# Attention, MoE and softplus MLP on one core: six late weight pieces every four units, second GEMM four units behind, abs ahead of gh

## The chip, the cores and the metric

The program runs on one core of one Trainium2 chip. The metric is device time in microseconds (us); lower is better. Five engines work side by side, each through its own list in order: PE (TensorE, matmuls; its weight loads are listed as PEld), DVE (VectorE), ACT (ScalarE), POOL (GpSimd) and SP, which here only issues DMAs.

## The reference, cut to what matters

Windowed attention, then a mixture of eight experts (the first MoE), then a dense MLP with softplus between its two GEMMs. The change lies in that last part, called the second MoE by the code.

```python
def _moe2_ref(x, w_in, w_out):          # x 2304x512, w_in 512x2048, w_out 2048x512
    h = x @ w_in
    g = np.maximum(h, 0.0) + np.log1p(np.exp(-np.abs(h)))
    return (g @ w_out).astype(np.float32)

def _moe_ref(x, w_gate, w_output_gate, w1, w2):
    ...
    for e in range(E):                  # 8 experts, a token goes to its best one
        ...
        h = np.maximum(x[mask] @ w1[e], 0.0)
        ye = h @ w2[e]
        out[mask] = gate_w[mask, None] * eom[mask, e, None] * ye
```

w_in and w_out arrive as 64-bit floats. The kernel reads them as pairs of 32-bit words and makes 32-bit floats of them with integer operations.

## The kernel before

**Precision.** Every GEMM is done with three matmuls: each operand is cut into a high part (a cast on ACT, names wh, gh, xh) and a low part (a subtraction on DVE, names wl, gl, xl), and high x high, high x low and low x high are summed in PSUM.

**Second MoE.** The 2304 tokens stand in 6 blocks b of 384, the 2048 hidden columns in 16 strips f of 128. A pair (b, f) is a unit; the list `steps` has 96 of them, blocks 0 and 1 interleaved in groups of four strips (units 0 to 31), blocks 2 to 5 after them. In the loop, round i issues on PE `gemm1` of unit i (12 matmuls of 384 columns into one of two buffers of PSUM, pg) and `gemm2` of unit i - LAG (9 matmuls of 512 columns into q); LAG is 3. Between them stands softplus, in three pieces, recorded in the order c of unit i - 2, a of unit i, b of unit i - 1:

- `softplus_a` (L1394): ACT takes u = |h| (L1399), u = exp(-u) (L1400) and l = relu(h) (L1401), the two reads of pg; DVE takes w = u + 1 (L1402) and the rounding error of that sum, u = (w - 1) - u (L1404).
- `softplus_b` (L1406): ACT takes w = ln w (L1408), DVE l = l + w (L1409) and l = l - u (L1411).
- `softplus_c` (L1415): ACT casts gh from l (L1417), DVE subtracts gl = l - gh (L732).

**Weights.** w_in and w_out of the second MoE come in 16 pieces of 128 x 1024: even pieces hold two strips of w_in, odd ones those of w_out. Pieces 0 to 7 are made 32-bit during the first MoE (`prep_tick`, every fifth step of experts 1 to 7, one 128 x 512 slice at a time: a load, |w| on ACT, four operations on DVE, a store), stored in DRAM as w_in32 and w_out32, and read back. Then they need a cast `hi_` and a subtraction `lo_` of 128 x 1024 each, at the unit that N_HL gives (16 there is unit 0). Pieces 8 to 15 are late: they are loaded as 64-bit words into two tiles wr each and converted during units 2 to 27 by `direct` in four steps, piece j at unit D_AT + D_STEP * (j - 8) + D_OFF[step]: steps 0 and 1 are |w| of one half on ACT into a tile cm (L168; the pool cm has one buffer), then four operations on DVE (L172, L178, L180, L182), put between the softplus operations by `aside`; step 2 casts both halves to wh on ACT (L816); step 3 subtracts wl, two halves, on POOL (L732 there).

**Buffers.** wr has five tiles. `load_next` issues the next load on SP when a piece's low part has been recorded; a late piece needs two tiles. Finished rows of q are copied to o by DVE or ACT and scattered to the output by an indirect DMA from POOL (L1440). After the last gemm1, END orders the matmuls of gemm2 that are left by strip and by third t of the block: before, the first third of block 5 is finished nine matmuls before the end, the second six, the last third at the end.

Of the kernel before, what the change touches and what calls it, by code (L numbers as in the profile page):

```python
# [21 lines left out]
P = 128  # L22
# [5 lines left out]
WARM = 28  # L28
NE_AT = ((6, 14), (7, 0), (7, 1), (7, 2))
X2_AT, X2_HL = (0, 3), ((6, 7, 8, 9), (12, 13, 14, 15))  # L30
N_HL = (8, 10, 12, 14, 16, 18, 20, 22)

D_AT, D_STEP, D_OFF = 2, 3, (0, 1, 3, 4)
XG = 6
IDX_AT, GATHER_AT = 8, 12
TR_AT = (5, 7, 8, 9)
# [6 lines left out]
def attn_moe_softplus_kernel(ctx: ExitStack, tc: tile.TileContext, q, k, v, w_gate, w_ogate, w1, w2, w_in, w_out, out, dbg=None):  # L43
# [25 lines left out]
    identb = const.tile([P, P], BF16, name="identb")  # L69
    upper = const.tile([P, P], BF16, name="upper")  # L70
    ones = const.tile([P, P], BF16, name="ones")
    wg = const.tile([P, NC, 32], F32, name="wg")
    rev = const.tile([P, NE], F32, name="rev")
    eidx = const.tile([P, NE], F32, name="eidx")
    ebase = const.tile([P, NE], BF16, name="ebase")
    pair = const.tile([P, NTL, 2], I32, name="pair")
    lg = const.tile([P, NTL, 2 * NE], F32, name="lg")
    cumb = const.tile([P, len(GROUPS) + 1, NE], BF16, name="cumb")
    tabi = const.tile([1, 40], I32, name="tabi")
    perm_sb = const.tile([P, NT // P, 2], I32, name="perm_sb")  # L80
# [69 lines left out]


    DIRECT = 8
    N_IN, N_OUT = DIRECT // 4, DIRECT // 4 * (PC // P)
    PREP = [(0, r_, c_) for r_ in range(DM // P) for c_ in range(N_IN)] + [(1, r_, 0) for r_ in range(N_OUT)]
    NPREP = len(PREP)
    prep_in, prep_t, prep_n = {}, {}, [0, 0, 0]
# [588 lines left out]
    pieces = {}  # L745

    def load_piece(r, j, e=None):
        if r == NE and j >= DIRECT:

            pieces[r, j] = []  # L750
            for h in range(2):
                if j % 2 == 0:
                    src = w_in.bitcast(I32)[256 * h : 256 * h + 256, 256 * j : 256 * j + 512].rearrange("(c p) f -> p c f", p=P)
                else:
                    src = w_out.bitcast(I32)[128 * (j - 1 + h) : 128 * (j - 1 + h) + 128].unsqueeze(1)
                t = K["wr"].tile([P, 1024], F32, tag="wr", name=f"wr{r}_{j}{h}").bitcast(I32)
                nc.sync.dma_start(t.rearrange("p (c f) -> p c f", c=src.shape[1]), src)
                pieces[r, j].append(t)
            return
        if r == NE:  # L760
            g = j // 2
            if j % 2 == 0:
                src = w_in32[:, 256 * g : 256 * g + 256].rearrange("(c p) f -> p c f", p=P)
            else:
                src = w_out32[256 * g : 256 * g + 256].rearrange("(c p) d -> p c d", p=P)
        elif j < 4:
            src = w1[ds(e, 1), :, 256 * j : 256 * j + 256].rearrange("o (c p) f -> p (o c) f", p=P)
        else:
# [27 lines left out]
    def direct(j, step):  # L796
# [18 lines left out]
            for h in range(2):  # L815
                nc.scalar.copy(d[2][:, hs[h]], w_[h])  # L816
        else:
            for h in range(2):
                sub(nc.gpsimd, d[3][:, hs[h]], w_[h], d[2][:, hs[h]])
                load_next()  # L820

    def piece_lo(r, j, eng=None):
        d = pieces[r, j]
# [215 lines left out]
    def load_next():  # L1039

        nload[1] += 1
        while nload[1] and nload[0] < len(order_):
            r, j = order_[nload[0]]
            two = r == NE and j >= DIRECT
            if two and nload[1] < 2:
                break
            if r not in er and r != NE:
# [259 lines left out]
        sub(nc.vector, x2[b][1][:, cs, :BT], x2[b, h], x2[b][0][:, cs, :BT])  # L1307


    for j, u in enumerate(N_HL):  # L1310
        last_rank.setdefault(u, []).append((hi_, NE, j))
        last_rank.setdefault(u + 1, []).append((lo_, NE, j))
    for b, at_ in enumerate(X2_HL):
# [59 lines left out]

    cctx = mctx
    K["wb"] = cctx.enter_context(tc.tile_pool(name="wb", bufs=1))
    K["cm"] = cctx.enter_context(tc.tile_pool(name="cm", bufs=1))
    sp_p = cctx.enter_context(tc.tile_pool(name="sp", bufs=2))
    g_p = cctx.enter_context(tc.tile_pool(name="g", bufs=3))
    o_p = cctx.enter_context(tc.tile_pool(name="o", bufs=3))
# [15 lines left out]
    def softplus_a(b, f):  # L1395
# [3 lines left out]
        nc.scalar.activation(u, ps, AF.Abs)  # L1399
        nc.scalar.activation(u, u, AF.Exp, scale=-1.0)  # L1400
        nc.scalar.activation(l, ps, AF.Relu)  # L1401
        nc.vector.tensor_scalar(w_, u, 1.0, None, ALU.add)  # L1402
        aside()
        nc.vector.scalar_tensor_tensor(u, w_, 1.0, u, ALU.subtract, ALU.subtract)  # L1404

    def softplus_b(b, f):  # L1406
        u, w_, l = sp[b, f]
        nc.scalar.activation(w_, w_, AF.Ln)  # L1408
        nc.vector.tensor_tensor(l, l, w_, ALU.add)  # L1409
        aside()  # L1410
# [113 lines left out]
```

## Time and profile before

| | |
|---|---|
| median of 3 runs (lowest, highest) | 814.38 us (814.18 to 817.77) |
| the profiled execution's own time | 815.12 us |
| its span in the trace | 813.5 us |
| busy in the span: PE, DVE, ACT, POOL | 95%, 70%, 58%, 17% |
| mean granted clock of PE | 0.981 |
| first MoE, first gemm to last | 158.6 to 390.7 us |
| second MoE, first gemm1 to last matmul | 390.8 to 802.9 us |

PE is named busy for 95% of the span, but its matmuls are pipelined and their ends are modelled, so a busy share hides small waits. A stretch is better read by how many matmuls began in it: the same 21 matmuls (12 and 9) make a unit all through the second MoE. The count behind PEld, one weight load for each matmul, serves for that.

### The profile page before, as it was taken

The page shows a single profiled execution, that of the slowest core. Times are in us where ns is not written, and L with a number is a line of the kernel's source. Part 1 is how long each engine was busy: PE and PEld are TensorE (multiplying, and loading weights), DVE is VectorE, ACT ScalarE, POOL GpSimd, SP SyncE. Part 2 cuts the span into 40 slices and gives each one's busy share as a digit, 9 for nine tenths or more (in the row PEclk, how much of TensorE's full clock was granted, in tenths as well). Part 3 has the DMA queues.
Part 4 walks back from the last instruction along what each step waited for, and adds up shares of the span by engine and source line. Part 5 has one row for each costly group of instructions (what it writes and reads, how often), then busy time and mean ns, then how long its engine had stood idle before and what let it go on. Part 6 is the DMA issues. An engine that isn't in the chain of part 4 may idle for free.

```text
span 813.5 us, 14993 instructions
## 1 busy us (share of the span) xinstructions
PE 769.4 (95%) x5542; PEld 689.8 (85%) x5543; DVE 566.0 (70%) x1112; ACT 471.8 (58%) x909; POOL 141.3 (17%) x170
## 2 busy tenths in 40 slices
PE   6998885999999999999989999999999999999994
PEld 5666664898999999999978888899999999999993
DVE  6867884653577887656798989867656656666662
ACT  4776542344655665566766676656656655655561
POOL 9814433121102001100012121210000001001001
PEclk8999998799999999999999999999999999999998
DMA  9996666255799998769431322310000001001000
GB/s 227 267 249 172 137 163 154 72 194 168 241 285 294 306 306 281 234 195 345 109 103 62 96 67 71 91 65 1 20 7 33 0 1 39 1 1 39 1 1 39
DMA packets 85887, 104.49 MB, mean 128 GB/s; under 512 B 30428, under 2 KB 61404, under 8 KB 85792
## 3 DMA queue, kind: packets, MB, share of 16 engines
q1 hardware_dynamic: 74496, 84.22, 35.9%
q0 software_dynamic: 5104, 13.40, 5.1%
q10 hardware_dynamic: 6192, 5.56, 2.0%
q8 instruction: 65, 1.06, 0.6%
q14 instruction: 30, 0.25, 0.1%
HBM read 83.98 MB, written 19.32 MB: 127 GB/s over the span
## 4 chain that ended last, share of the span: by engine, by line
PE 61%; DVE 11%; issue 9%; ACT 4%; DMA 2%; POOL 1%; ACTq 0%; POOLq 0%; DVEq 0%; SPq 0%
PE q L1433 5%; PE pg L895 5%; PE pg L896 5%; PE pg L894 5%; PE q L1431 5%; PE q L1432 5%; PE ph L890 3%; PE ph L892 3%; PE ph L891 3%; PE py L890 3%; PE py L891 3%; PE py L892 3%; DVE l L1411 2%; DVE l L1409 1%; PE py L894 1%
## 5 line engine op out<-in xcount | busy, mean ns | idle before, releaser
L895 PE MATMUL pg<-xlm,wh 128*128 128x384 f32 x384 | 129.7, 338 | 0.0
L894 PE MATMUL pg<-xhm,wh 128*128 128x384 f32 x384 | 129.4, 337 | 0.1
L896 PE MATMUL pg<-xhm,wl 128*128 128x384 f32 x384 | 129.3, 337 | 0.0
L1433 PE MATMUL q<-wh,gl 128*128 128x512 f32 x288 | 114.3, 397 | 3.8 <-DVE gl L732 3.8
L1431 PE MATMUL q<-wh,gh 128*128 128x512 f32 x288 | 114.2, 397 | 1.4 <-ACT gh L1417 0.9
L1432 PE MATMUL q<-wl,gh 128*128 128x512 f32 x288 | 113.2, 393 | 0.0
L732 DVE TENSOR_TENSOR wl<-wr,wh 128x1024 fp32r<-128x1024 f32 x72 | 87.6, 1218 | 32.9 <-ACT wh L787 32.9
L1417 ACT CAST gh<-l 128x384 fp32r<-128x384 f32 x96 | 49.2, 512 | 100.9 <-DVE l L1411 100.9
L732 DVE TENSOR_TENSOR gl<-l,gh 128x384 fp32r<-128x384 f32 x96 | 56.6, 590 | 41.2 <-ACT gh L1417 39.6
L787 ACT CAST wh<-wr 128x1024 fp32r<-128x1024 f32 x72 | 75.0, 1047 | 15.2 <-ACT y L917 6.0
L894 PEld LDWEIGHTS pg<-xhm,wh 128*128 128x128 f32 x384 | 72.1, 188 | 4.3 <-ACT l L1401 0.4
L895 PEld LDWEIGHTS pg<-xlm,wh 128*128 128x128 f32 x384 | 72.0, 188 | 3.8
L1433 PEld LDWEIGHTS q<-wh,gl 128*128 128x128 f32 x288 | 54.0, 188 | 22.1 <-DVE gl L732 10.1
L1402 DVE TENSOR_SCALAR w<-u 128x384 f32<-128x384 f32 x96 | 34.7, 361 | 54.5 <-ACT u L1400 53.8
L896 PEld LDWEIGHTS pg<-xhm,wl 128*128 128x128 f32 x384 | 72.1, 188 | 0.0
L1440 POOL DMA_INDIRECT out_dram<-o,perm_sb x18 | 18.6, 1034 | 271.9 <-DVE o L259 137.4
L1431 PEld LDWEIGHTS q<-wh,gh 128*128 128x128 f32 x288 | 54.1, 188 | 11.9 <-ACT gh L1417 4.2
L1411 DVE TENSOR_TENSOR l<-l,u 128x384 f32<-128x384 f32 x96 | 62.2, 648 | 2.8
L1432 PEld LDWEIGHTS q<-wl,gh 128*128 128x128 f32 x288 | 54.1, 188 | 8.2
L1399 ACT ACTIVATE u<-pg 128x384 f32<-128x384 f32 x96 | 46.9, 488 | 22.3 <-PE pg L896 21.9
L890 PE MATMUL ph<-xh,wh 128*128 128x392 f32 (+5 forms) x192 | 58.5, 305 | 0.9 <-ACT y L917 0.9
L890 PE MATMUL py<-hh,wh 128*128 128x312 f32 (+8 forms) x192 | 58.5, 304 | 0.0
(205 smaller groups left out, 1763.6 us busy)
## 6 DMA issues: line engine op xcount, KB each, us to landing
wr<-in_moe_w_dram SPq DMA_DIRECT2D x64, 512.0 KB, 5.3
raw<-in_q_dram SPq DMA_DIRECT2D x8, 576.0 KB, 5.8
raw<-in_k_dram SPq DMA_DIRECT2D x8, 576.0 KB, 7.5
x2r<-yT_dram SPq DMA_DIRECT2D x12, 384.0 KB, 3.6
vP<-in_v_dram SPq DMA_DIRECT2D x16, 272.0 KB, 8.3
praw<-in_moe_w_in_dram SPq DMA_DIRECT2D x8, 512.0 KB, 5.0
praw<-in_moe_w_out_dram SPq DMA_DIRECT2D x8, 512.0 KB, 5.5
wr<-in_moe_w_in_dram SPq DMA_DIRECT2D x8, 512.0 KB, 4.0
```

Source lines behind the costliest of these rows:

```text
L732: e.tensor_tensor(lo, src, hi.bitcast(F32), ALU.subtract)
L787: (eng or nc.scalar.copy)(d[1], d[0])
L890: nc.tensor.matmul(ps if wide else ps[:, :cut], wh, xh if wide else xh[:, :cut], start=wide, stop=False, skip_group_check=True)
L891: nc.tensor.matmul(ps[:, :cut], wh, xl[:, :cut], start=False, stop=False, skip_group_check=True)
L894: nc.tensor.matmul(ps, wh, xh, start=(first and i == 0), stop=False)
L895: nc.tensor.matmul(ps, wh, xl, start=False, stop=False)
L896: nc.tensor.matmul(ps, wl, xh, start=False, stop=(last and i == k - 1))
L1411: nc.vector.tensor_tensor(l, l, u, ALU.subtract)
L1417: nc.scalar.copy(gT[b, f][0], l)
L1431: nc.tensor.matmul(acc[b, t], gh[:, ts_], wh, start=(f == 0), stop=False)
L1432: nc.tensor.matmul(acc[b, t], gh[:, ts_], wl, start=False, stop=False)
L1433: nc.tensor.matmul(acc[b, t], gl[:, ts_], wh, start=False, stop=(f == NF - 1))
```

## The change

- Pieces 9 and 11 are no longer late. N_OUT rises by four, so four more 128 x 512 slices of w_out go through `prep_tick` in the first MoE; the two pieces are then read from w_out32 and split by `hi_` and `lo_` at units 8 and 14. Late are the six pieces 8, 10, 12, 13, 14, 15, one every four units from unit 4 on, their last two steps in the same round.
- cm has two buffers. Room comes from wg and lg, which move from the pool const to a pool that closes after the attention.
- The two subtractions of wl of a late piece go from POOL to DVE, one `aside` each.
- w = u + 1 is done on ACT (a copy with a bias of 1) for the first 28 units, on DVE after.
- l = l - u is taken in `softplus_a`, ahead of the logarithm.
- The order within a round is a, c, b: |h| stands in front of gh. LAG is 4, and END is written anew: the first third of block 5 is finished twelve matmuls before the end, the second still six.

```diff
-N_HL = (8, 10, 12, 14, 16, 18, 20, 22)
-D_AT, D_STEP, D_OFF = 2, 3, (0, 1, 3, 4)
+N_HL = {0: 8, 1: 10, 2: 12, 3: 14, 4: 16, 5: 18, 6: 20, 7: 22, 9: 24, 11: 30}
+D_AT, D_STEP, D_OFF = 4, 4, (0, 1, 3, 3)
...
-    N_IN, N_OUT = DIRECT // 4, DIRECT // 4 * (PC // P)
+    N_IN, N_OUT = DIRECT // 4, DIRECT // 4 * (PC // P) + 4
+    LATE = [j for j in range(DIRECT, 16) if j not in (9, 11)]
...
-            for h in range(2):
-                sub(nc.gpsimd, d[3][:, hs[h]], w_[h], d[2][:, hs[h]])
-                load_next()
+            def subs():
+                for h in range(2):
+                    sub(nc.vector, d[3][:, hs[h]], w_[h], d[2][:, hs[h]])
+                    load_next()
+                    yield 1
+            side.append(subs())
...
-    K["cm"] = cctx.enter_context(tc.tile_pool(name="cm", bufs=1))
+    K["cm"] = cctx.enter_context(tc.tile_pool(name="cm", bufs=2))
+    LAG = 4
...
         nc.scalar.activation(l, ps, AF.Relu)
-        nc.vector.tensor_scalar(w_, u, 1.0, None, ALU.add)
+        if steps.index((b, f)) < 28:
+            nc.scalar.activation(w_, u, AF.Copy, bias=1.0)
+        else:
+            nc.vector.tensor_scalar(w_, u, 1.0, None, ALU.add)
         aside()
         nc.vector.scalar_tensor_tensor(u, w_, 1.0, u, ALU.subtract, ALU.subtract)
+        aside()
+        nc.vector.tensor_tensor(l, l, u, ALU.subtract)
 
     def softplus_b(b, f):
         u, w_, l = sp[b, f]
         nc.scalar.activation(w_, w_, AF.Ln)
         nc.vector.tensor_tensor(l, l, w_, ALU.add)
-        aside()
-        nc.vector.tensor_tensor(l, l, u, ALU.subtract)
         aside()
...
-    LAG = 3
-    END = {0: [(NF - 3, (0, 1)), (NF - 2, (0, 1)), (NF - 3, (2,))], 2: [(NF - 1, (0, 1)), (NF - 2, (2,)), (NF - 1, (2,))]}
+    END = {0: [(NF - 4, (0, 1, 2)), (NF - 3, (0, 1)), (NF - 2, (0,)), (NF - 3, (2,))], 2: [(NF - 1, (0,)), (NF - 2, (1,)), (NF - 1, (1,)), (NF - 2, (2,)), (NF - 1, (2,))]}
...
-            order_sp = [(2, softplus_c), (0, softplus_a), (1, softplus_b)]
+            order_sp = [(0, softplus_a), (2, softplus_c), (1, softplus_b)]
```

**ACT while a late piece is converted.** In the names, u0_5 is u of block 0, strip 5, cm10_1 is |w| of the second half of piece 10, pg the result of gemm1. Before, from one half's |w| to the next:

```order
L168 ACTIVATE cm10_0_8827<-wr8_100_8735 128x512
L1417 CAST gh1_3_8851<-l1_3_8774 128x384
L1399 ACTIVATE u0_5_8856<-pg0_5_8829 128x384
L1400 ACTIVATE u0_5_8856<-u0_5_8856 128x384
L1401 ACTIVATE l0_5_8858<-pg0_5_8829 128x384
L1408 ACTIVATE w0_4_8813<-w0_4_8813 128x384
L168 ACTIVATE cm10_1_8876<-wr8_101_8737 128x512
L1417 CAST gh0_4_8900<-l0_4_8814 128x384
```

The same piece of ACT's list now:

```order
L167 ACTIVATE cm10_0_8842<-wr8_100_8750 128x512
L1406 ACTIVATE u0_5_8871<-pg0_5_8849 128x384
L1407 ACTIVATE u0_5_8871<-u0_5_8871 128x384
L1408 ACTIVATE l0_5_8873<-pg0_5_8849 128x384
L1410 ACTIVATE w0_5_8872<-u0_5_8871 128x384
L1427 CAST gh1_3_8882<-l1_3_8778 128x384
L1420 ACTIVATE w0_4_8824<-w0_4_8824 128x384
L167 ACTIVATE cm10_1_8890<-wr8_101_8752 128x512
```

The cast gh of the unit two back stood first in a round, ahead of the reads of pg; it now stands behind them and behind the new sum w.

**DVE at the end of a late piece.** Before, DVE's list where piece 8 is being finished (its wl is on POOL) and piece 9 begins:

```order
L732 TENSOR_TENSOR gl1_0_8715<-l1_0_8629,gh1_0_8714 128x384
L172 TENSOR_SCALAR cm9_0_8687<-cm9_0_8687 128x512
L1402 TENSOR_SCALAR w1_2_8720<-u1_2_8719 128x384
L178 TENSOR_SCALAR cm9_0_8687<-cm9_0_8687 128x512
L1404 SCALAR_TENSOR_TENSOR u1_2_8719<-w1_2_8720,u1_2_8719 128x384
L1409 TENSOR_TENSOR l1_1_8674<-l1_1_8674,w1_1_8673 128x384
L180 SCALAR_TENSOR_TENSOR wr8_90_8642<-wr8_90_8642,cm9_0_8687 128x512
L1411 TENSOR_TENSOR l1_1_8674<-l1_1_8674,u1_1_8672 128x384
L182 SCALAR_TENSOR_TENSOR wr8_90_8642<-wr8_90_8642 128x512
```

Now, where piece 8 is finished and piece 9, prepared, is split:

```order
L733 TENSOR_TENSOR wl8_8_8792<-wr8_80_8526,wh8_8_8791 128x512
L1414 SCALAR_TENSOR_TENSOR u0_4_8823<-w0_4_8824,u0_4_8823 128x384
L733 TENSOR_TENSOR wl8_8_8792<-wr8_81_8528,wh8_8_8791 128x512
L1416 TENSOR_TENSOR l0_4_8825<-l0_4_8825,u0_4_8823 128x384
L733 TENSOR_TENSOR gl1_2_8837<-l1_2_8732,gh1_2_8836 128x384
L1421 TENSOR_TENSOR l1_3_8778<-l1_3_8778,w1_3_8777 128x384
L733 TENSOR_TENSOR wl8_9_8796<-wr8_9_8586,wh8_9_8795 128x1024
```

The two wl of piece 8 came onto DVE, the sum w left it, and l = l - u moved up by a round.

**DVE at the border of two experts of the first MoE.** pw18 is slice 18 of `prep_tick`, wl6_3 a low weight of expert rank 6, hl6_0 the low part of its first hidden strip, which frees that strip's buffer of PSUM. Before, DVE's list there:

```order
L732 TENSOR_TENSOR wl6_3_7267<-wr6_3_6827,wh6_3_7266 128x1024
L908 SCALAR_TENSOR_TENSOR hl6_0_7401<-ph6_0_7374,hh6_0_7400 128x280
L732 TENSOR_TENSOR wl6_4_7372<-wr6_4_6932,wh6_4_7371 128x1024
L878 UNCONDITIONAL_BRANCH
L908 SCALAR_TENSOR_TENSOR hl6_1_7434<-ph6_1_7407,hh6_1_7433 128x280
```

Now:

```order
L733 TENSOR_TENSOR wl6_3_7285<-wr6_3_6833,wh6_3_7284 128x1024
L177 TENSOR_SCALAR pw17_7107<-pw17_7107 128x512
L179 SCALAR_TENSOR_TENSOR pw17_7107<-praw17_6527,pw17_7107 128x512
L181 SCALAR_TENSOR_TENSOR pw17_7107<-praw17_6527,pw17_7107 128x512
L171 TENSOR_SCALAR pw18_7333<-pw18_7333 128x512
L177 TENSOR_SCALAR pw18_7333<-pw18_7333 128x512
L179 SCALAR_TENSOR_TENSOR pw18_7333<-praw18_6599,pw18_7333 128x512
L181 SCALAR_TENSOR_TENSOR pw18_7333<-praw18_6599,pw18_7333 128x512
L171 TENSOR_SCALAR pw19_7403<-pw19_7403 128x512
L914 SCALAR_TENSOR_TENSOR hl6_0_7433<-ph6_0_7406,hh6_0_7432 128x280
```

Eight operations of two slices came in a row between the last weights of one expert and the first hidden strip of the next.

## Rows read from the trace of the kernel before

**Rows 1.** Stretches of the second MoE: length, busy us of each engine (instructions)
```profile
core 0: us, PE busy (x) PEld busy (x) DVE busy (x) ACT busy (x) POOL busy (x), PEclk, DMA share, GB/s
401.76:516.89 115.13, 109.91 (x526) 92.64 (x525) 105.26 (x194) 75.47 (x159) 23.20 (x16) 1.00 0.26 79
525.28:792.41 267.13, 267.13 (x1345) 242.62 (x1344) 172.22 (x339) 156.44 (x339) 15.74 (x15) 1.00 0.05 19
700.61:733.70 33.09, 33.09 (x169) 30.26 (x168) 21.64 (x43) 19.28 (x41) 0.00 (x0) 1.00 0.01 1
```

**Rows 2.** Waits from 401.76 to 516.89: who for whom: us, times, longest
```profile
ACT gh L1417 <- DVE l L1411: 24.4, 17, 2.8
ACT cm L168 <- DVE wr L180: 14.2, 8, 1.8
PEld q L1433 <- DVE gl L732: 9.8, 19, 1.3
```

**Rows 3.** DVE's groups in that stretch: xcount | busy us, mean ns | idle before
```profile
L1411 DVE TENSOR_TENSOR l<-l,u 128x384 f32<-128x384 f32 x26 | 23.1, 890 | 0.3
L732 DVE TENSOR_TENSOR gl<-l,gh 128x384 fp32r<-128x384 f32 x25 | 17.0, 682 | 6.1 <-ACT gh L1417 4.5 <-PE pg L896 1.2
L1409 DVE TENSOR_TENSOR l<-l,w 128x384 f32<-128x384 f32 x26 | 15.4, 593 | 0.0
L182 DVE SCALAR_TENSOR_TENSOR wr<-wr 128x512 int32<-128x512 int32 x16 | 10.9, 682 | 0.0
L1402 DVE TENSOR_SCALAR w<-u 128x384 f32<-128x384 f32 x25 | 8.9, 356 | 3.1 <-ACT u L1400 2.7
L172 DVE TENSOR_SCALAR cm<-cm 128x512 f32<-128x512 f32 x16 | 6.7, 418 | 0.0
L732 DVE TENSOR_TENSOR wl<-wr,wh 128x1024 fp32r<-128x1024 f32 x3 | 3.7, 1218 | 0.0
```

**Rows 4.** The first of those groups from 560 to 740 us, without late pieces
```profile
L1411 DVE TENSOR_TENSOR l<-l,u 128x384 f32<-128x384 f32 x44 | 24.5, 557 | 1.5
```

**Rows 5.** ACT's groups in the stretch of rows 1
```profile
L1408 ACT ACTIVATE w<-w 128x384 f32<-128x384 f32 x25 | 12.9, 515 | 0.0
L168 ACT ACTIVATE cm<-wr 128x512 f32<-128x512 f32 x15 | 10.1, 675 | 14.2 <-DVE wr L180 14.2
L816 ACT CAST wh<-wr 128x512 fp32r<-128x512 f32 x16 | 9.7, 657 | 0.0
L787 ACT CAST wh<-wr 128x1024 fp32r<-128x1024 f32 x2 | 2.1, 1047 | 0.0
```

**Rows 6.** Timeline of one late piece: start us, length us, [idle before <-releaser]
```profile
457.75 2.89 POOL L732 TENSOR_TENSOR wl<-wr,wh 128x512 fp32r<-128x512 f32 x2 [10.59 <-ACT wh L816]
457.83 1.66 DVE L1411 TENSOR_TENSOR l<-l,u 128x384 f32<-128x384 f32 x1
463.57 0.68 ACT L168 ACTIVATE cm<-wr 128x512 f32<-128x512 f32 x1 [1.80 <-DVE wr L180]
```

**Rows 7.** Timeline at the start: first two |h|, last matmul of the fourth gemm1
```profile
393.75 0.48 ACT L1399 ACTIVATE u<-pg 128x384 f32<-128x384 f32 x1
395.17 0.49 ACT L1399 ACTIVATE u<-pg 128x384 f32<-128x384 f32 x1
399.33 0.34 PE L896 MATMUL pg<-xhm,wl 128*128 128x384 f32 x1
```

**Rows 8.** Two stretches of the first MoE, columns as in rows 1
```profile
322.00:334.00 12.00, 11.81 (x91) 11.57 (x89) 11.03 (x18) 8.71 (x17) 0.00 (x0) 1.00 0.70 220
347.00:359.00 12.00, 12.00 (x107) 12.00 (x106) 8.16 (x13) 9.24 (x16) 0.00 (x0) 1.00 0.62 193
```

**Rows 9.** Timeline of the last copy and the last two scatters
```profile
802.92 0.58 ACT L1437 COPY o<-q 128x512 f32<-128x512 f32 x1 [1.45 <-PE q L1433]
803.00 0.96 POOL L1440 DMA_INDIRECT out_dram<-o,perm_sb  x1 [0.31 <-issue]
804.27 0.96 POOL L1440 DMA_INDIRECT out_dram<-o,perm_sb  x1 [0.30 <-issue]
```

More of the change, by code (lines that the diff above doesn't have):

```diff
@@ L71, in attn_moe_softplus_kernel @@
     ones = const.tile([P, P], BF16, name="ones")
-    wg = const.tile([P, NC, 32], F32, name="wg")
     rev = const.tile([P, NE], F32, name="rev")
@@ L76, in attn_moe_softplus_kernel @@
     pair = const.tile([P, NTL, 2], I32, name="pair")
-    lg = const.tile([P, NTL, 2 * NE], F32, name="lg")
     cumb = const.tile([P, len(GROUPS) + 1, NE], BF16, name="cumb")
@@ L215, in attn_moe_softplus_kernel @@
     per_p = [None, actx.enter_context(tc.tile_pool(name="per1", bufs=1))]
+    wg = per_p[1].tile([P, NC, 32], F32, name="wg")
+    lg = per_p[1].tile([P, NTL, 2 * NE], F32, name="lg")
     mask_w = per_p[1].tile([P, 2, 64], BF16, name="mask_w")
@@ L747, in load_piece @@
     def load_piece(r, j, e=None):
-        if r == NE and j >= DIRECT:
+        if r == NE and j in LATE:
             pieces[r, j] = []
@@ L1043, in load_next @@
             r, j = order_[nload[0]]
-            two = r == NE and j >= DIRECT
+            two = r == NE and j in LATE
             if two and nload[1] < 2:
@@ L1307, in x2_lo @@
         sub(nc.vector, x2[b][1][:, cs, :BT], x2[b, h], x2[b][0][:, cs, :BT])
-    for j, u in enumerate(N_HL):
+    for j, u in N_HL.items():
         last_rank.setdefault(u, []).append((hi_, NE, j))
@@ L1465, in attn_moe_softplus_kernel @@
         x2_at(b, *((s0 + 8, s0 + 12, s0 + 13, s0 + 13, s0 + 14) if b == 2 else (s0 + 4, s0 + 8, s0 + 9, s0 + 10, s0 + 11)))
-    for j in range(DIRECT, NF):
+    for k_, j in enumerate(LATE):
         for s in range(4):
-            post.setdefault(D_AT + D_STEP * (j - DIRECT) + D_OFF[s], []).append((direct, j, s))
+            post.setdefault(D_AT + D_STEP * k_ + D_OFF[s], []).append((direct, j, s))
     for i in range(len(steps) + LAG):
```

## The prediction

> **What bounds the kernel now.** I read the stretches first, since PE is named busy nearly everywhere. From unit 31 on, 1344 matmuls begin in 267.13 us [rows 1], one every 0.1988 us, 4.17 us for a unit of 21. That is PE's own pace: it has no gap there, and DVE is busy for 172 of the 267 us, ACT for 156. From unit 4 to unit 28, the same count of 525 matmuls (25 units) takes 115.13 us. At the later pace they would take 525 x 0.1988 = 104.4 us. So **10.8 us** are lost there, all of it while late pieces are converted, and all at a granted clock of 1.00. The reader is to see that the busy share would have hidden this: 109.91 of 115.13 us.
>
> Then the waits of that stretch [rows 2]. PE's weight loads wait for gl from DVE; ACT waits for DVE twice over, 24.4 us for l ahead of gh and 14.2 us for the second |w| of a piece, which needs the one buffer cm. Nothing waits for a DMA. So the loop is DVE to ACT to DVE, and DVE is its heavy part: busy for 105.26 us [rows 1] of work that PE would want done in 104.4.
>
> Last, why DVE is that heavy. Its three softplus operations of 128x384 with two operands, 77 of them, took 23.1 + 17.0 + 15.4 = 55.5 us [rows 3]; at the 0.557 us that the same operation takes where no piece is converted [rows 4] they are 42.9. The 12.6 us between lie where POOL subtracts: one of them takes 1.66 us beside POOL's pair of 2.89 [rows 6]. A piece also makes ACT stand 1.80 us for cm [rows 6], with gh, the reads of pg and exp queued behind it.
>
> **The change, part by part.** The sum is made for the profiled execution, 815.12 us, which is 0.74 above the median.
>
> DVE in the stretch. Busy 105.3; off go the 12.6 of POOL's subtractions, 8.9 of w = u + 1 [rows 3], and two of eight pieces, each 4 x 0.418 + 4 x 0.682 = 4.4 (L178 is like L172 and L180 like L182), 8.8 in all. On come twelve subtractions of 128x512: the trace has none on DVE alone, but it lies between 0.557 [rows 4] and half of 1.218 or the 0.682 of L182 [rows 3]; with the last, 8.2. Two more lo_ of 1.218 make 2.4. Sum 85.6 us, 82% of PE's 104.4.
>
> ACT in the stretch. Busy 75.5 [rows 1]; on come 25 sums. A copy with a bias isn't in the trace; the logarithm, from SBUF to SBUF in the same shape, takes 0.515 [rows 5], and no ACT instruction of this shape differs from it much, so 12.9. Off go two pieces of 2 x 0.675 + 2 x 0.657 = 2.7 [rows 5], 5.3; on come two casts of double width, 2.1. Sum 85.2 us, again 82%.
>
> So both fit under PE with a fifth to spare, and what is late next is PE itself. Three edits make the loop loose as well as light: with two buffers cm the 14.2 us go, because a half waits only for the half before the last; gh now stands behind the reads of pg, so its wait no longer delays them; and gemm2 four units behind gives gl a whole round, 4.17 us, more. l - u ahead of the logarithm costs nothing, it is the same operation, and it shortens what follows the logarithm by 0.557. The SP queue carries fewer loads than before; a load waits there for a tile wr, and behind it stands only the next one, needed four units later. I take the 10.8 us as **gone but for 0.5**: units 4 to 11 hold three of the stretch's four hi_ (pieces 6, 7 and 9) beside the conversion of 8 and 10, so ACT has 8 x 3.41 there and nearly 2 more, 29 of 33.4 us, and waits come in bursts. Bounds 0 and 4 for this rest.
>
> The start. PE now does five gemm1 before its first gemm2, and gemm1 of unit 4 needs relu of unit 2. ACT's first |h| begins at 393.75 and the second 1.42 later [rows 7], so three triples take 4.3; two sums and one logarithm between them 3 x 0.515, and hi_ of piece 5 1.0 [rows 5]: relu of unit 2 ends by 400.6, and a little earlier as neighbours overlap; I take 400.4. PE is free at 399.33 + 0.17 = 399.5 [rows 7], so it waits about 0.9. Against the kernel before it begins that gemm1 at 400.4 with nine matmuls (half a unit, 2.1) still owed, where before began it at 401.76 (the bound of the stretch) without: 400.4 + 2.1 - 401.8 = **+0.7** (0 to 1.5).
>
> The first MoE. Four slices more: 4 x 2.2 = 8.8 us of DVE, 4 x 0.68 of ACT [rows 3, 5], and on SP four loads and four stores, with the experts' weight loads queued behind each store's wait for DVE. It falls between 322 and 359 us. The hard place is the border of ranks 5 and 6, where two slices now follow each other on DVE ahead of the first hl; from 347 to 359 DVE would be filled: 8.16 [rows 8] plus two slices less a clamp, 4.0, of 12.0. The trace has this once already, at the border of ranks 4 and 5: DVE 11.03 of 12.00, and PE lost 0.19 [rows 8]. If nothing covered DVE, all 8.8 would show; PE's three buffers of PSUM for these strips cover it, and I take **+0.5** (0 to 2.5).
>
> The end. The last copy ends at 802.92 + 0.58 = 803.50, but its scatter starts at 804.27, because POOL needs 1.27 for each of three [rows 9]. The first third now finishes three matmuls (0.6) earlier, so POOL's three begin as much earlier, and the last starts at about 803.6: **-0.7** (0 to -0.8; more than the copy's end at 803.50 allows it can't be). Before that, nine more matmuls stand in front of the last strip, so softplus of units 94 and 95 stays covered.
>
> The rest, units 31 to 95, changes order only: PE runs there without gaps, whatever ACT does first.
>
> Sum: -10.8 + 0.5 + 0.7 + 0.5 - 0.7 = **-9.8 us**; 815.12 becomes 805.3, and on the scale of the median 814.38 becomes 804.6.
>
> A rule that speaks against one edit stands in the Trainium skill, "ScalarE: Activation LUTs", section "Rules for kernel authors": an add is to be done on VectorE and not on ScalarE. The trace agrees on the size, 0.356 on DVE [rows 3] against 0.515 for a like ACT instruction. By the rule w would stay on DVE, which would then hold 85.6 + 8.9 = 94.5 of 104.4 us, ACT 72.3. What the rule warns of here is the first rival.
>
> **The rivals.**
>
> *ACT becomes the bound, in part.* A unit's ACT work in the stretch is 85.2 / 25 = 3.41 us. If ACT still waits for DVE by some amount in each unit, PE is slowed once that passes 4.17 - 3.41 = 0.76 us; before, it waited (24.4 + 14.2) / 25 = 1.54 [rows 2]. For it speaks that gh still needs l from DVE one round back and that DVE cannot begin a round before ACT has made w. Against it: the wait for cm has lost its cause, and gh's has 1.9 us more, since four instructions now stand in front of it. At 1.0 us a unit, two thirds of the old wait, 25 x 0.24 = 6 us would stay lost in place of the 0.5: 810.1, between 807.5 and 812.
>
> *Slower: ACT's waits stay.* The same place, with ACT's wait undiminished at 1.54: a unit takes 3.41 + 1.54 = 4.95, 25 of them 123.8 us, 8.6 over before, with the other terms (0.7 + 0.5 - 0.7) +9.1: 823.5. It is slower than before from a wait of 1.2 us a unit (115.13 / 25 - 3.41). Only the loop through DVE could keep it, and DVE is to lose a fifth of its load.
>
> *The first MoE pays.* Weight loads of rank 6 and 7 slip behind the four stores, and PE stands for half of the 8.8 us: +4.4 in place of +0.5, 808.5. Against it, PE lost next to nothing with sixteen such slices in ranks 1 to 5.
>
> *The change doesn't do what it says.* If the loss weren't DVE's load but the pace of PE beside busy engines, nothing would come back: +0.5, 814.9. Against it, rows 2 name the waits, and 115.13 / 104.4 is DVE's own share of load.
>
> **How the numbers follow.** Forecast 804.6, chance 0.69: its own range 801.5 to 807.5 comes from the bounds above, and from PE's pace, which isn't the same in all units: 168 matmuls in 33.09 us is 0.1970 [rows 1], so 1.0 us of the stretch and up to 2 of the rest hang on what sets it. ACT in part 0.15; the first MoE 0.05; nothing comes back 0.07; slower 0.04. To hold 8 in 10 the range must reach into the first rival: 800.8 to 810.0. A difference of 0.5% (4.1 us) is about what a measurement can tell here; faster than 810.3 are the forecast, the first MoE's case and more than half of the first rival: 0.84; within 0.5% 0.12; slower 0.04.
>
> **What would show it.** Units 4 to 28 at 4.1 to 4.25 us each, 525 matmuls in 103.5 to 106; no DVE operation of 1.6 us, POOL without work from 400 to 520; ACT's wait for cm gone, and its wait for l under 10 us; DVE and ACT busy for some 82% there; PE's only wait of note before gemm1 of unit 4, under 1.5 us; less than 1 us lost at 347; the last scatter within 0.2 us of the last copy. I am wrong if the stretch holds its 115 us with the POOL work gone (then DVE's load wasn't the cause), if ACT is busy for over 95%, or if the first gemm1 begins over 2 us later than at 390.8.

## The result and the profile after

The changed kernel takes **804.71 us** (median of 6 runs, 803.44 to 807.45), the kernel before on the same chip 815.32 (6 runs, 814.18 to 819.61): ratio 0.9866, interval 0.9837 to 0.9894. The forecast was 804.6. The profiled execution of after took 803.44 us with a span of 801.8, against 815.12 and 813.5.

The time of the two profiled executions, cut at the same points of the program (first and last matmuls of the stages and units):

| piece | before | after | difference | forecast |
|---|---|---|---|---|
| start to first gemm of the first MoE | 158.64 | 156.74 | -1.9 | 0 |
| first MoE, to the first gemm1 of the second | 232.15 | 233.11 | +0.96 | +0.5 |
| units 0 to 3 | 10.97 | 9.26, with 2.1 still owed | +0.4 | +0.7 |
| units 4 to 28 | 115.13 | 104.43 | -10.7 | -10.3 |
| unit 29 to the last matmul | 285.61 | 287.67, of which 2.1 were owed | 0.0 | 0 |
| last matmul to the end of the span | 11.0 | 10.55 | -0.5 | -0.7 |

The first line lies ahead of everything that the change touches. Over all the profiles of this study that point falls anywhere from 156.7 to 172.3 us, much of it from chip to chip; it is scatter and no part of the effect. Without it the terms make -9.8, the sum of the prediction. The table is why most comparisons below go by the length of a stretch and not by the whole time: the units of the second MoE repeat within a tenth of a microsecond, the whole run does not.

The stretch of units 4 to 28 in the kernel after, columns as in rows 1:

```profile
399.11:503.54 104.43, 104.43 (x526) 94.84 (x526) 86.01 (x169) 86.41 (x186) 0.00 (x0) 1.00 0.23 75
```

PE is busy from end to end; POOL does nothing; DVE and ACT stand at 82 and 83%. The waits in it, the answer to rows 2:

```profile
DVE u L1414 <- ACT w L1410: 17.2, 19, 1.5
ACT u L1406 <- PE pg L902: 16.7, 18, 1.5
DVE w L1412 <- ACT u L1407: 1.5, 1, 1.5
PEld pg L900 <- ACT l L1408: 0.7, 1, 0.7
ACT w L1410 <- DVE l L1421: 0.4, 1, 0.4
```

ACT no longer waits for cm, and for l once, 0.4 us. It waits for PE (|h| for its gemm1), DVE waits for ACT, and only one wait reaches PE, at gemm1 of unit 4. The direction of the chain has turned: PE leads, the others follow. The groups of DVE that answer to rows 3:

```profile
L1414 DVE SCALAR_TENSOR_TENSOR u<-w,u 128x384 f32<-128x384 f32 x26 | 14.5, 556 | 17.2 <-ACT w L1410 17.2
L1416 DVE TENSOR_TENSOR l<-l,u 128x384 f32<-128x384 f32 x26 | 14.4, 554 | 0.3
L733 DVE TENSOR_TENSOR wl<-wr,wh 128x512 fp32r<-128x512 f32 x11 | 7.5, 684 | 0.0
```

l - u is back at 0.554 us (it was 0.890 on average in rows 3), and a subtraction of 128x512 takes 0.684 on DVE. The sum on ACT:

```profile
L1410 ACT ACTIVATE w<-u 128x384 f32<-128x384 f32 x26 | 13.4, 517 | 0.5 <-DVE l L1421 0.4
```

The two prices without a row ahead of the result, 0.682 and 0.515, were right to 0.002. At the start PE waits before gemm1 of unit 4 (0.37 us here and 0.16 of pipelining ahead of it), and in the first MoE the border of ranks 5 and 6, where eight operations of three slices (pw17 to pw19) stand in DVE's list, costs 0.7 us where [rows 8] before shows none:

```profile
399.11 0.44 PE L900 MATMUL pg<-xhm,wh 128*128 128x384 f32 x1 [0.37 <-ACT l L1408]
```
```profile
345.00:357.00 12.00, 11.30 (x97) 11.10 (x97) 11.43 (x20) 8.61 (x16) 0.00 (x0) 1.00 0.77 261
```
```profile
PE ph L896 <- DVE hl L914: 0.7, 1, 0.7
```

At the end, against [rows 9]: the last copy ends at 792.22, the last scatter starts at 792.51, 0.29 us later, where before it was 0.77.

```profile
791.25 0.96 POOL L1450 DMA_INDIRECT out_dram<-o,perm_sb  x1 [0.51 <-DVE o L260]
791.63 0.59 ACT L1447 COPY o<-q 128x512 f32<-128x512 f32 x1 [2.13 <-PE q L1443]
792.51 0.96 POOL L1450 DMA_INDIRECT out_dram<-o,perm_sb  x1 [0.30 <-ACT o L1447]
```

So far all seems to go by the book. What the numbers don't tell is whether DVE's load was the cause, or something else that the same edits changed. The experiments ask that.

### The profile page after: what moved, and what is told of

It reads as the page before. It is cut to its first block, busy times and chain, and to the rows that moved or that the text cites. A ratio compares the mean times of both kernels' runs of the same rounds, so it can differ in the third digit from the quotient of the medians.

```text
span 801.8 us, 15124 instructions
## 1 busy us (share of the span) xinstructions
PE 764.0 (95%) x5542; PEld 690.7 (86%) x5543; DVE 548.5 (68%) x1098; ACT 479.3 (60%) x935; POOL 119.9 (15%) x154
## 4 chain that ended last, share of the span: by engine, by line
PE 69%; issue 8%; DVE 5%; ACT 3%; DMA 2%; POOL 0%; ACTq 0%; SPq 0%; POOLq 0%; DVEq 0%
PE pg L900 7%; PE pg L901 7%; PE pg L902 7%; PE q L1442 7%; PE q L1441 7%; PE q L1443 7%; PE py L896 3%; PE py L897 3%; PE py L898 3%; PE ph L896 3%; PE ph L898 2%; PE ph L897 2%; PE ph L900 1%; PE ph L902 1%; PE ph L901 1%
## 5 line engine op out<-in xcount | busy, mean ns | idle before, releaser
L733 DVE TENSOR_TENSOR wl<-wr,wh 128x1024 fp32r<-128x1024 f32 (+1 forms) x86 | 98.2, 1144 | 30.7 <-ACT wh L788 30.6
L1443 PE MATMUL q<-wh,gl 128*128 128x512 f32 x288 | 112.6, 391 | 0.0
L788 ACT CAST wh<-wr 128x1024 fp32r<-128x1024 f32 x74 | 77.2, 1047 | 15.1 <-ACT y L923 5.2
L1412 DVE TENSOR_SCALAR w<-u 128x384 f32<-128x384 f32 x68 | 24.6, 362 | 84.7 <-ACT u L1407 84.2
L1414 DVE SCALAR_TENSOR_TENSOR u<-w,u 128x384 f32<-128x384 f32 x96 | 53.7, 560 | 21.6 <-ACT w L1410 19.3
L1416 DVE TENSOR_TENSOR l<-l,u 128x384 f32<-128x384 f32 x96 | 53.5, 557 | 7.7 <-ACT w L1420 0.5
L897 PE MATMUL py<-hl,wh 128*128 128x312 f32 (+4 forms) x192 | 57.3, 299 | 0.1
```

Source lines behind the costliest of these rows:

```text
L733: e.tensor_tensor(lo, src, hi.bitcast(F32), ALU.subtract)
L788: (eng or nc.scalar.copy)(d[1], d[0])
L897: nc.tensor.matmul(ps[:, :cut], wh, xl[:, :cut], start=False, stop=False, skip_group_check=True)
L1443: nc.tensor.matmul(acc[b, t], gl[:, ts_], wh, start=False, stop=(f == NF - 1))
```

## The experiments

Each is one profiled run unless said otherwise; "stretch" is always the 525 matmuls of units 4 to 28. Lengths in us, and beside the whole time that of the kernel before on the same chip:

| kernel | units 0 to 3 | stretch | whole | before there |
|---|---|---|---|---|
| before | 10.97 | 115.13 | 815.12 | |
| after | 9.26 | 104.43 | 803.44 | 815.32 |
| after, POOL subtracts | 9.16 | 104.43 | 813.58 | 821.8 |
| after, one buffer cm | 9.25 | 104.44 | 813.3 | 821.8 |
| after, w on DVE | 8.67 | 104.32 | 815.78 | 828.76 |
| after, eight late pieces | 9.23 | 105.13 | 818.53 | 828.76 |
| after, gh first | 10.56 | 106.48 | 820.01 | 828.76 |
| after, LAG 3 | 13.83 | 105.16 | 825.48 | 828.76 |
| before, subtractions on DVE | 10.84 | 113.26 | 821.16 | 821.8 |
| before, two buffers cm | 10.94 | 113.56 | 825.28 | 821.8 |
| before, order and LAG 4 | 9.53 | 118.39 | 819.49 | 816.52 |
| after, one DVE operation more | 10.69 | 125.37 | 832.37 | 816.52 |
| after, two more | 11.18 | 140.03 | 847.56 | 816.52 |
| eight late pieces, w on DVE at first | 8.69 | 105.70 | 807.19 | 816.52 |

With LAG 4 half a unit of matmuls, 2.1 us, is still owed when units 0 to 3 are over.

### Undoing single edits in the kernel after

**POOL subtracts again.**

```diff
...
-                    sub(nc.vector, d[3][:, hs[h]], w_[h], d[2][:, hs[h]])
...
+                sub(nc.gpsimd, d[3][:, hs[h]], w_[h], d[2][:, hs[h]])
...
```

> The changed kernel, with one edit undone: the subtractions of wl are on POOL again, recorded right behind the casts. Theory: DVE gives 8.2 us of subtractions away and is held for six pieces x 1.6 = 9.5 us, 87 us of 104.4, so PE does not feel it: units 4 to 28 in 104.4 to 105.5 us, DVE operations of 1.6 us back. Rival (POOL's subtractions are the loss): 6 x 0.9 us a piece comes back, 109 us or more.

```profile
409.17:513.60 104.43, 104.43 (x525) 94.84 (x526) 89.14 (x158) 86.61 (x186) 17.80 (x12) 1.00 0.25 76
```

104.43 us, to the hundredth the same, with POOL busy for 17.8 us and DVE for 3 more. In the changed kernel this edit is worth nothing.

**One buffer cm again.**

```diff
-    K["cm"] = cctx.enter_context(tc.tile_pool(name="cm", bufs=2))
+    K["cm"] = cctx.enter_context(tc.tile_pool(name="cm", bufs=1))
```

> The changed kernel, with one edit undone: cm has one buffer again. Theory: DVE has 86 us of work for 104.4, so a wait of ACT for cm of up to 1.8 us in six pieces, 11 us, fits into ACT's 18 us of slack; the stretch of units 4 to 28 takes 104.4 to 105.5 us. Rival (the buffer is what the change lives by): 107 us or more, with PE waiting for gl.

```profile
ACT cm L167 <- DVE wr L179: 11.1, 6, 2.4
```

The wait is back with 11.1 us, and the stretch takes 104.44. A wait of up to 2.4 us on ACT reaches nobody here.

**w = u + 1 on DVE in all units.**

```diff
-        if steps.index((b, f)) < 28:
+        if steps.index((b, f)) < 0:
```

> The changed kernel with w = u + 1 on DVE in all units, as before. Theory: DVE 86 + 8.9 = 95 us, ACT 86.4 - 12.9 = 73.5, PE 104.4: units 4 to 28 in 104.4 to 106 us, and since ACT has less in front of relu of unit 2, PE waits up to 0.5 us less before gemm1 of unit 4. Rival (DVE was so near its limit that this edit is needed): 108 us or more.

```profile
411.67:515.99 104.32, 104.32 (x526) 94.74 (x526) 94.09 (x196) 77.22 (x161) 0.00 (x0) 1.00 0.25 76
```

DVE at 90% and the stretch as short as before it. PE does not wait at unit 4 at all: units 0 to 3 take 8.67 us in place of 9.26. The sum on ACT is thus a small loss of 0.6 us at the start. The rule of the Trainium skill that the prediction weighed ("ScalarE: Activation LUTs", "Rules for kernel authors") is right for this kernel, though only where units begin without a stock of work.

**Eight late pieces, one every three units, and no further slices in the first MoE.**

```diff
-N_HL = {0: 8, 1: 10, 2: 12, 3: 14, 4: 16, 5: 18, 6: 20, 7: 22, 9: 24, 11: 30}
+N_HL = {0: 8, 1: 10, 2: 12, 3: 14, 4: 16, 5: 18, 6: 20, 7: 22}
-D_AT, D_STEP, D_OFF = 4, 4, (0, 1, 3, 3)
+D_AT, D_STEP, D_OFF = 2, 3, (0, 1, 3, 4)
...
-    N_IN, N_OUT = DIRECT // 4, DIRECT // 4 * (PC // P) + 4
-    LATE = [j for j in range(DIRECT, 16) if j not in (9, 11)]
+    N_IN, N_OUT = DIRECT // 4, DIRECT // 4 * (PC // P)
+    LATE = list(range(DIRECT, 16))
```

> The changed kernel with eight late pieces every three units from unit 2, as before; pieces 9 and 11 are not prepared in the first MoE. All else stays changed. Theory (load): DVE gets 86 + 8.8 + 2.7 - 2.4 = 95 us for PE's 104.4, ACT 90, so in rounds with a conversion both are close to PE's pace: 104.6 to 107.5 us for units 4 to 28; the first MoE 1 us shorter. Rival (the number of late pieces was the loss): 109 us or more.

```profile
413.61:518.74 105.13, 104.91 (x526) 94.65 (x526) 95.07 (x187) 90.19 (x193) 0.00 (x0) 1.00 0.27 85
```

The stretch gets 0.7 us longer, the first MoE 1.0 shorter (232.12). Over the whole study the first MoE takes 232.0 to 232.9 (mean 232.4) in the six kernels without the four slices and 233.1 to 234.8 (mean 234.0) in the eight with them: their price is 1.6 us, which is more than they save.

**gh ahead of |h| again.**

```diff
-            order_sp = [(0, softplus_a), (2, softplus_c), (1, softplus_b)]
+            order_sp = [(2, softplus_c), (0, softplus_a), (1, softplus_b)]
```

> The changed kernel, with softplus of a round recorded in the order c, a, b as before (gh in front of |h|). Theory: gh waits for DVE again, up to 2 us a round, with the reads of pg behind it, but ACT and DVE have a fifth to spare and gemm2 is four units behind: units 4 to 28 in 104.4 to 106.5 us, ACT's wait for l back. Rival (the order is what freed the loop): 108 us or more.

```profile
413.37:519.85 106.48, 106.40 (x525) 93.98 (x525) 87.29 (x163) 81.90 (x177) 0.00 (x0) 1.00 0.23 71
```
```profile
ACT gh L1427 <- DVE l L1421: 21.7, 21, 1.8
```

Here ACT waits for l almost as long as in rows 2, with DVE at 82%, and the stretch loses 2.0 us; units 0 to 3 lose 1.3. So ACT's wait for l is no matter of DVE's load: it comes from the order.

**Second GEMM three units behind**, with the END of before.

```diff
-    LAG = 4
+    LAG = 3
...
```

> The changed kernel, with the second GEMM three units behind again and END as before. In the changed kernel's trace gl of a unit is ready 8.0 to 8.9 us after the next unit's gemm1 ends in rounds with a conversion; with three units PE wants it after 8.35. Theory (the fourth unit is slack that heavy rounds need): PE waits some 0.3 us in about half of the units, 25 units (4 to 28) in 105.5 to 109 us, and the start is 0.4 us quicker. Rival (load alone decides, and it is 82%): 104.4 to 105.

The stretch is 105.16, 0.7 longer, a little under the 105.5 that was expected at least; unit 4 alone makes it so (4.96 for 4.30), the other 24 units together lose 0.1. The expectation had the start 0.4 us shorter; units 0 to 3 take 13.83 in place of 9.26 + 2.1, so 2.5 more. PE meets its first gemm2 before gh and gl are there, and then the clock falls. Two matmuls of the timeline and four windows:

```profile
413.03 0.50 PE L1441 MATMUL q<-wh,gh 128*128 128x512 f32 x1 [1.18 <-ACT gh L1427]
414.28 0.50 PE L1443 MATMUL q<-wh,gl 128*128 128x512 f32 x1 [0.53 <-DVE gl L733]
415.54 0.63 PE L1441 MATMUL q<-wh,gh 128*128 128x512 f32 x1
```
```profile
411.60:414.60 3.00, 1.29 (x5) 0.59 (x4) 1.97 (x5) 2.97 (x8) 0.00 (x0) 1.00 0.44 147
414.60:416.80 2.20, 2.20 (x7) 1.69 (x6) 2.17 (x4) 2.16 (x5) 0.00 (x0) 0.60 0.00 0
416.80:420.00 3.20, 3.20 (x15) 3.14 (x14) 1.03 (x3) 0.40 (x2) 0.00 (x0) 0.74 0.43 164
420.00:424.00 4.00, 4.00 (x22) 3.64 (x21) 2.21 (x5) 3.08 (x7) 0.00 (x0) 1.00 0.00 0
```

After 3 us in which PE was busy for 1.29, the granted clock is 0.60 on average for 2.2 us, so mostly the lower of its two levels (1.2 and 2.4 GHz). From unit 29 on this kernel loses 5.2 us more (290.77 for 287.67 - 2.1). All of it lies in units 31, 35, 51, 67 and 83, which take 4.97 to 5.72: each comes right after the last gemm2 of a block, while DVE and ACT copy the finished rows of q, and PE waits for gh or gl. So the fourth unit of distance is worth next to nothing inside the stretch, and much at the start and at the ends of blocks.

### Doing single edits in the kernel before

**Subtractions on DVE alone.**

```diff
...
-                sub(nc.gpsimd, d[3][:, hs[h]], w_[h], d[2][:, hs[h]])
...
+                    sub(nc.vector, d[3][:, hs[h]], w_[h], d[2][:, hs[h]])
...
```

> The kernel before, with one edit: the two subtractions of wl of a late piece are done on DVE, one between softplus operations, in place of POOL. Read: time of units 4 to 28 (525 matmuls; 115.1 us before, 104.4 after). Theory (DVE's load against PE's pace, with the loop DVE to ACT to DVE on top): DVE loses the 12.6 us of holding and gains 16 x 0.68 = 10.9, so it stays at some 103.5 us of work for PE's 104.4, and ACT still waits 1.8 us for cm once a piece: 109 to 114 us. Rival (what POOL's subtractions do to DVE is the whole loss): 104.4 to 106 us.

```profile
409.69:522.95 113.26, 107.24 (x527) 94.01 (x526) 103.54 (x211) 77.08 (x163) 0.00 (x0) 1.00 0.24 76
```
```profile
ACT gh L1422 <- DVE l L1416: 23.0, 17, 2.9
ACT cm L168 <- DVE wr L180: 12.4, 8, 1.8
```

It gives back 1.9 us of the 10.7, within the 109 to 114 expected, and both waits of rows 2 stay.

**Two buffers cm alone**; two small tiles, wg and lg, move to another pool to make room.

```diff
...
-    K["cm"] = cctx.enter_context(tc.tile_pool(name="cm", bufs=1))
+    K["cm"] = cctx.enter_context(tc.tile_pool(name="cm", bufs=2))
```

> The kernel before, with one edit: cm has two buffers, and wg and lg move to the pool that closes after the attention to make room. Theory: DVE keeps its 105.3 us of work for PE's 104.4, so the stretch of units 4 to 28 keeps at least half of the loss: 109 to 113 us, ACT's wait for cm (14.2 us) gone and its wait for l of about the same size or longer. Rival (the one buffer cm makes the loss, since gh and the reads of pg stand behind it): 104.4 to 106.5 us.

```profile
413.56:527.12 113.56, 109.19 (x527) 93.36 (x526) 105.15 (x194) 75.52 (x159) 23.22 (x16) 1.00 0.27 80
```
```profile
ACT gh L1417 <- DVE l L1411: 37.0, 25, 2.9
```

It gives back 1.6 us; the stretch lies just above the 109 to 113 that were expected. The 14.2 us of waiting for cm are gone, and nearly all of them (12.6) have moved to gh's wait for l, now in each of 25 rounds. Whoever adds up waits as if each could be removed by itself counts them twice.

**Order and distance alone: |h| ahead of gh, gemm2 four units behind, the new END.**

```diff
-    LAG = 3
+    LAG = 4
...
-            order_sp = [(2, softplus_c), (0, softplus_a), (1, softplus_b)]
+            order_sp = [(0, softplus_a), (2, softplus_c), (1, softplus_b)]
```

> The kernel before, with only the looseness of the change: gemm2 four units behind with END as changed, and the order a, c, b. DVE keeps all its work, POOL its subtractions, cm its one buffer, eight late pieces. Theory (load): DVE was busy for 105.3 us of the stretch and PE wants 104.4, so units 4 to 28 take at least 105.3 and, with ACT's waits, 106 to 110 us. Rival 1 (order and lag are the whole gain, DVE's load is none of it): 104.3 to 105.2. Rival 2 (without a lighter DVE they give nothing): 113 us or more.

```profile
401.21:519.60 118.39, 110.83 (x526) 93.09 (x526) 99.17 (x193) 75.41 (x160) 23.67 (x16) 1.00 0.25 74
```

The load theory's 106 to 110 is out. The number lies in the second rival's range (113 or more), but that rival had the two edits give nothing, and the stretch is **longer** than before by 3.3 us, with nearly every unit at some 4.7 us. The waits and one round of ACT and DVE from the timeline say why:

```profile
ACT u L1399 <- DVE l L1411: 27.0, 17, 2.9
PEld pg L894 <- ACT l L1401: 18.9, 25, 1.1
```
```profile
485.20 0.49 ACT L1399 ACTIVATE u<-pg 128x384 f32<-128x384 f32 x1 [2.43 <-DVE l L1411]
486.29 0.36 DVE L1402 TENSOR_SCALAR w<-u 128x384 f32<-128x384 f32 x1 [0.58 <-ACT u L1400]
486.68 0.56 DVE L1404 SCALAR_TENSOR_TENSOR u<-w,u 128x384 f32<-128x384 f32 x1
487.16 0.55 DVE L732 TENSOR_TENSOR gl<-l,gh 128x384 fp32r<-128x384 f32 x1
487.63 0.55 DVE L1409 TENSOR_TENSOR l<-l,w 128x384 f32<-128x384 f32 x1
488.21 1.60 DVE L1411 TENSOR_TENSOR l<-l,u 128x384 f32<-128x384 f32 x1
489.91 0.49 ACT L1399 ACTIVATE u<-pg 128x384 f32<-128x384 f32 x1 [0.76 <-DVE l L1411]
```

|h| does not need l. It needs a free tile u, of which there are two, and l = l - u is the last that reads the one it is to write. So the round closes on itself: |h| and exp on ACT, w, u, gl, l + w, l - u on DVE, and then the next |h|. One turn here takes 489.91 - 485.20 = 4.71 us, where PE needs 4.17 for a unit, and PE waits for relu in each of the 25 rounds. With gh in front it is gh that waits for the same l - u. The order changes who waits, not for what.

### How much load does DVE bear?

**One and two more DVE operations in each of the units 0 to 27 of the kernel after.** They add work only; the tile `extra` is read by nobody. The diff is that with one.

```diff
         nc.vector.tensor_tensor(l, l, w_, ALU.add)
+        if steps.index((b, f)) < 28:
...
+            for _ in range(1):
+                nc.vector.tensor_tensor(sp["extra"], u, u, ALU.add)
```

> The changed kernel with one more DVE operation of 128x384 in each of the first 28 units, behind l + w, on a tile of its own that nothing reads (work added to no end). DVE was busy for 86.0 us of 104.4; one operation more per unit starts 0.47 us after its neighbour, 25 x 0.47 = 12, so 98 us. Theory (PE loses time only when DVE's work nears PE's): units 4 to 28 in 104.4 to 106.5 us. Rival (the loop's length, not the load, sets it): 25 x 0.47 us shows in part at once, 108 us or more.

> The same with two more DVE operations per unit: 86.0 + 24 = 110 us for PE's 104.4. Theory: DVE is the bound again, units 4 to 28 in 109 to 114 us, DVE busy for over 95% of it, PE's weight loads waiting for gl from DVE as in the kernel before. Rival (DVE's load was not the bound): under 106 us.

```profile
406.75:532.12 125.37, 111.99 (x526) 94.28 (x526) 95.78 (x188) 81.96 (x177) 0.00 (x0) 0.99 0.20 60
406.46:546.49 140.03, 112.58 (x526) 94.18 (x526) 109.75 (x213) 81.99 (x177) 0.00 (x0) 0.99 0.18 54
```
```profile
ACT u L1406 <- DVE extra L1426: 42.6, 24, 2.7
```

Both are far above the 104.4 to 106.5 and 109 to 114 of the load theory; the first is where its rival, the length of the loop, had it (108 or more). One operation of 0.55 us a unit makes the stretch 21 us longer, and DVE is then busy for 95.78 of 125.37 us: 76%, less than in the kernel after. With the sum on DVE, above, nearly as much DVE work (94 us) fitted into 104.3. **Load alone is not it.** The round of the first one, ACT and DVE:

```profile
479.57 0.49 ACT L1406 ACTIVATE u<-pg 128x384 f32<-128x384 f32 x1 [1.75 <-DVE extra L1426]
481.44 0.56 DVE L1414 SCALAR_TENSOR_TENSOR u<-w,u 128x384 f32<-128x384 f32 x1 [1.63 <-ACT w L1410]
482.25 0.55 DVE L1416 TENSOR_TENSOR l<-l,u 128x384 f32<-128x384 f32 x1
483.79 0.55 DVE L1421 TENSOR_TENSOR l<-l,w 128x384 f32<-128x384 f32 x1
484.26 0.55 DVE L1426 TENSOR_TENSOR extra<-u 128x384 f32<-128x384 f32 x1
484.90 0.49 ACT L1406 ACTIVATE u<-pg 128x384 f32<-128x384 f32 x1 [2.10 <-DVE extra L1426]
```

The added operation happens to read u, one round later than l - u does in this kernel. That gives the tile back its late reader, and with it the closed round: 484.90 - 479.57 = 5.33 us. It was meant as load and was a hold on a buffer; as a measure of load it is spoilt, as a test of the loop it is the clearest run of the study.

### A version meant to beat the change

**Eight late pieces as above, no slices more in the first MoE, and w on DVE in units 0 to 3** (4 runs). To the diff with eight pieces comes

```diff
-        if steps.index((b, f)) < 28:
+        if 4 <= steps.index((b, f)) < 28:
```

> The changed kernel without two of its parts: eight late pieces every three units (nothing more is prepared in the first MoE), and w = u + 1 on DVE for units 0 to 3, on ACT for 4 to 27, on DVE after. By the two runs that undid these singly: PE's wait before gemm1 of unit 4 gone (-0.6 us against the changed kernel), first MoE 232.1 us instead of 233 to 234.8 (-1 to -2.5), units 4 to 28 in 105.0 to 105.4 us (+0.7): 1 to 2.4 us faster than the changed kernel, a ratio to before of 0.982 to 0.987. Rival (the two edits lean on each other: eight pieces with w on DVE in front fill DVE): units 4 to 8 slower by over 1 us, no gain.

```profile
403.05:508.75 105.70, 105.03 (x527) 94.56 (x527) 95.75 (x190) 89.72 (x191) 0.00 (x0) 1.00 0.26 85
```

807.19 us against 816.52: ratio 0.989, 0.985 to 0.993, above the 0.982 to 0.987 that was expected. Units 0 to 3 gain 0.6 as expected (8.69), the first MoE 0.2 by the single profile, but the stretch loses 1.3 in place of 0.7 (unit 9 takes 4.93, unit 26 4.67). It is faster than before and not shown to be faster than the change.

## Why the prediction was right, and where its reason was wrong

**The stretch: right to 0.4 us, by a reason that fell.** The prediction saw that 10.8 us lie there, that nothing but the waits between DVE and ACT holds PE, and that PE's own pace would be what is left; all three stand. Its next step was that DVE is "the heavy part", with 105.26 us of work that PE would want done in 104.4. By its own numbers that is 0.9 us too much, and could not make 10.8 us; the 115.13 / 104.4 that it calls DVE's share of load is the stretch against PE's own pace; DVE's is 105.26 / 104.4. About 95 us of DVE work have been run in four kernels, and the stretch took

| kernel | DVE busy | stretch |
|---|---|---|
| after, w on DVE | 94.09 | 104.32 |
| after, eight late pieces | 95.07 | 105.13 |
| eight late pieces, w on DVE in units 0 to 3 | 95.75 | 105.70 |
| after, one operation more that reads u | 95.78 | 125.37 |

What decides is a closed round: ACT's early instruction waits for DVE's last, and DVE's first waits for ACT. Such a round has a length of its own. Where it is shorter than PE's 4.17 us a unit, PE sets the pace and the others wait for it, as in the waits of after; where it is longer, the units pay the difference. In the kernel with one DVE operation more nearly every unit pays. In the kernel before three turns, from the gh that starts at 437.16 us to the one at 450.67, take 4.50 us each on average, and PE's loss gathers in units 5 to 8 (4.95 to 5.30 us) and then in every third, 10 to 28 (4.97 to 5.17), while the others take 4.17 to 4.23. That DVE was busy for 91% of that stretch does not show, then, that its load was the limit.

**The step that failed** is the sentence on l - u: ahead of the logarithm it "costs nothing" and shortens what follows by 0.557. It costs nothing indeed, but it does more than shorten: it lets go of tile u a round earlier, so that |h| waits for nobody but PE, and it leaves gh waiting for l + w alone, with four ACT instructions in front of it. Two pairs show the weight. |h| in front with l - u last gives 118.4, l - u ahead with gh in front 106.5, both 104.4, neither 115.1. These four differ in other edits too. The subtractions and the buffer cm were worth 1.9 and 1.6 in the kernel before and 0.0 in the kernel after; the sum on ACT (0.1) and two pieces fewer (0.7) were priced in the kernel after alone. Sizes taken there, where the round is shorter than PE's unit, do not say what the same edits are worth in a round that is longer, so the 10.7 us cannot be divided by exclusion. The move of l - u was not run alone, nor undone alone. The two runs with a late reader of u allow an estimate of undoing it in the kernel after, since DVE would then have the work of the first of these runs less one operation: the second added operation made the units 0.59 us longer on average (140.03 against 125.37), and as much less than 125.37 leaves a stretch of 110.7, or 113.5 if no unit is let fall below its time in the kernel after. That is 6 to 9 us over 104.4. It is an inference, not a measurement, and holds with the sum on ACT, which stands in that round too; whether the lighter edits together would have brought the round of before under PE's pace without the move was not tried. Nor was a DVE operation added that reads something other than u; at what load DVE itself would hold PE is not known beyond 94 of 104.3 us.

**"Three edits make the loop loose"**: of the three, two buffers cm were worth nothing here; the four units of distance 0.7 in the stretch, all in unit 4 behind the fall of the clock, but 2.5 at the start and 5.2 after it; gh behind |h| 2.0.

**The sizes of DVE's and ACT's work** (85.6 and 85.2 forecast, 86.0 and 86.4 measured) came out well, partly because two errors cancel. The busy time of a window counts overlapping instructions once, while mean durations count each in full. Summed by groups, DVE of after is 97.5 us for a window that says 86.0. The forecast took sums of durations off a window's busy time and put others on; what was too much on the one side was too much on the other.

**Rivals.** That ACT's waits stay, at 1.0 or 1.54 us a unit, did not come true, but it was no idle fear: the kernels with |h| waiting for u show it, 118.4 where that rival priced 123.8. The bound of 1.2 us of waiting a unit was set too simply, since what the waiting costs depends on whether the round is closed. That nothing comes back is out, and so is the first MoE's +4.4.

**The other terms.** The start +0.4 for +0.7: the fifth gemm1 begins at 399.11, 9.26 us after the first, where 400.4 - 390.8 = 9.6 was worked out: relu of unit 2 came that much earlier, as ACT's neighbours overlap more than was allowed for. The first MoE +0.96 for +0.5, and the mean over all kernels says 1.6: this term was mis-sized, at the very border that the prediction named, by the wait of ph for hl. The end -0.5 for -0.7: the second scatter waits 0.51 us for its rows from DVE, and the third starts one turn of POOL, 1.26, behind it, which leaves it 0.29 after the copy in place of 0.1; all kernels with the new END need 10.5 to 10.6 us from the last matmul to the end, those with the old one 11.0.

## What to carry to other kernels

When two engines wait for each other in every round, write down the round as a cycle, with the tiles that an instruction must find free as well as the data that it reads, and compare its length with the pace of the engine that should lead; busy shares on the cycle say nothing about how much work it still bears. Look for the last reader of each tile with few buffers: moving that one instruction forward may be worth more than taking work off the engine that runs it (6 to 9 us here by the estimate above, which no run has confirmed). Test a load theory by adding work that touches no tile of the cycle, since an added reader changes the cycle itself.

## What the runs showed of the hardware

- **The clock after short waits.** PE stood for 1.7 us of a stretch of 3.0 at the start of the kernel with LAG 3; the granted clock was then 0.60 for 2.2 us and 0.74 for 3.2 us, and a matmul of 512 columns took up to 0.63 us (0.39 at a granted clock of 1.00). That is 2.2 x 0.40 = 0.9 us of the 2.9 by which units 0 to 3 are longer than in the kernel before, and 3.2 x 0.26 = 0.8 us in unit 4, as much as it loses there.
- **PE's pace has more than one value.** With no wait in sight a unit takes 4.13 us in some runs of units (16 to 19, 40 to 47, 72 to 79), 4.19 to 4.21 in others (20 to 23, 53 to 63) and 4.16 or 4.17 in a few, and a unit that does not wait repeats its value, mostly to 0.01 us, in every kernel with the same LAG and on every chip of the study. With LAG 3 the units of 4.13 begin one unit earlier, at 39 and 71, where the same gemm2 stands, and end at 47 and 79 as well. What sets the values was not found.
- **A wait on ACT of 11 us in sum can be free.** With one buffer cm, ACT stands for 11.1 us in the stretch and PE loses 0.01.
